# Strassen loop of a two-mixer kernel: token preparation gets call places of its own, masked rows a step of their own

## The chip, the cores and the metric

The kernel runs on one core of a Trainium2 chip. The metric is the device time of one execution in microseconds (us). TensorE is written PE (its weight loads PEld), VectorE DVE, ScalarE ACT, GpSimd POOL and SyncE SP.

## The reference

Pooled attention, then two mixers, over 8 batches of 576 tokens with 512 channels:

```python
attn = softmax(q @ mean8(k).T / 8) @ mean8(v)
x = attn laid out as (8, 576, 512)
u = x + (x.T @ U @ V).T
x1 = u + relu(u @ w1a) @ w2a
u2 = x1 + real(fft(fft(x1, axis=tokens), axis=channels))
un = (u2 - mean(u2)) / sqrt(var(u2) + 1e-6)
out = u2 + relu(un @ w1b) @ w2b
```

All of it is held to float32 precision: the matmuls take operands split into a high and a low part (`hi`, `lo`), so one product takes two or three matmuls.

## The kernel before

An opening and a first loop do attention, the first mixer's low-rank part and six of the nine 512-token blocks of its feed-forward layer. Then comes the **Strassen loop**, at line 1592: twelve blocks `seq[k]`, three of the first feed-forward layer (phase 0) and nine of the second (phase 1), with `NPR` = 8 turns `p` each, so 96 turns. A turn makes the seven Strassen products of one pair of 128-column slices of the hidden layer and the second layer of the turn before (`prev`). PE's order within a turn is written out by hand: products 0 and 1, `st2_a(prev, 0)`, `tick(0)`, products 2 and 3, `st2_a(prev, 1)`, `tick(1)`, products 4 and 5, `st2_a(prev, 2)`, `tick(2)`, product 6, `st2_a(prev, 3)`, `tick(3)`. The even products go to PSUM bank `h0`, the odd ones to `h1`, and DVE and ACT empty a bank before the next product may write it.

DVE's own work of a turn has a fixed order: `sa<-h,sa` after product 1 (product 3 waits for it), `hl<-sb` for the second layer, `sb<-h,sb` after product 4 (product 6 waits for it), `sa<-h,sa`, `sb<-sb`, `sa<-sa`, then `sb<-sa` and `hl<-sa` after product 6. PE, ACT and DVE run in program order (`manual_schedule`); SP and POOL are ordered by the scheduler.

Other work is cut into steps by Python generators, called lanes. `step(name)` (line 1346) runs one lane to its next `yield`, and what it issues stands at that place of every engine's queue. Two lanes run in the Strassen loop:

- `d`, the spectral lane (`lane_d`, `Dft.run`, line 747): the two Fourier transforms of one batch, residual and normalisation. A batch is twelve steps that form sums and differences of rows (three row groups, four steps each), one that masks the last rows (line 841) and in the same step makes the first stage group on PE (`stage`, seven matmuls), three with a further stage group, two for the extra column `px`, one with the first group of the second transform (`second`, thirteen matmuls), and for each of two or three row groups: differences (`S`, `E`), four additions (lines 940 to 943), two `bn_stats` (line 964), mean and variance, reciprocal root and first scaling, second scaling with the next `second`. Batch 0 runs in the first loop, batches 1 to 7 in the Strassen loop. After each pair of batches `state["u2"]` says how many rows of `un` are there.
- `p`, the preparation of the next block's operands (`prep_a`, line 1074): three steps that issue loads (`ul`, four DMAs each), five that transpose a tile on DVE (line 1122), copy high parts on ACT (line 1071) and subtract low parts on DVE (line 1072, shown as L121), then six with additions and subtractions for the Strassen operands, and a last one with two subtractions: fifteen calls.

`tick(i)` calls `swap()` (which replaces the second-layer weights, turns 17 to 31), one step of `d` and one of `p`. `place()` in `prep_a` lets the lane rest at `tick(2)`, once its loads are issued, so the preparation has three working calls a turn, at ticks 0, 1 and 3. It begins at the top of turn 0 of a block, or the first later turn at which `ready_for(k + 1)` holds; at turn 6 `until` runs all lanes until the preparation is done. In turn 0 DVE also adds the residual of the block just finished (`ur`, four additions, one behind each `st2_a`).

Of the kernel before, what the change touches and what calls it, by code (L numbers as in the profile page):

```python
# [61 lines left out]
def kernel(  # L62
# [663 lines left out]
    class Dft:  # L726
# [20 lines left out]
        def run(self, b, group):  # L747
# [47 lines left out]
            for i in range(3):  # L795
                f, r, n = fr
                if i < 2 and two():
                    fr = loads(i + 1)
                if low:
                    low()  # L800
                s = tl("S")
                e = tl("E")
                add(nc.vector, s[:n], f[:n], r[:n])
                yield
                sub(nc.vector, r[:n], f[:n], r[:n])
                nc.gpsimd.tensor_copy(e[:n, 0:1], s[:n, 0:1])
                nc.gpsimd.memset(e[:n, 511:512], 0.0)
                yield
                sub(nc.vector, e[:n, 256:511], r[:n, 1:256], r[:n, 256:511])
                add(nc.vector, e[:n, 1:256], s[:n, 1:256], s[:n, 256:511])  # L810
                if i < 2 and fr[0] is f:
                    fr = loads(i + 1)
                yield
                c2 = s[:n, 511:512].to_broadcast([n, 64])
                xe = tl(f"xe{i}", (128, 96 if i < 2 else 64), F32R)
                if i < 2:
                    xh, xl = tl(f"xh{i}", dt=F32R), tl(f"xl{i}", dt=F32R)
                    nc.scalar.activation(out=xh, in_=e, func=ACTF.Copy)
                    nc.scalar.activation(out=xe[:, 0:64], in_=c2, func=ACTF.Copy)

                    def low(xh=xh, xl=xl, xe=xe, e=e, c2=c2):
                        sub(nc.vector, xl, e, xh.bitcast(F32))
                        sub(nc.vector, xe[:, 64:96], c2[:, 0:32], xe[:, 0:32].bitcast(F32))
                    X.append((xh, xl))
                    XE.append(xe)
                    yield
                    if not two():
                        low()
                        low = None
                        yield  # L830
                else:
                    m = self.sm
                    both = []
                    for h, y, q in ((xe, c2, f[:, 0:64]), (None, e, r)):
                        h = h or tl("S", dt=F32R)
                        nc.scalar.activation(out=h[:n], in_=y[:n], func=ACTF.Copy)
                        nc.vector.tensor_scalar(out=q[:n], in0=y[:n], scalar1=m[:n, 0:1], scalar2=None, op0=ALU.mult)
                        both.append((h, q))
                    yield
                    for h, q in both:  # L840
                        nc.vector.scalar_tensor_tensor(out=h[:n], in0=h[:n].bitcast(F32), scalar=m[:n, 1:2], in1=q[:n], op0=ALU.mult, op1=ALU.add)  # L841
                    X.append((h,))
                    XE.append(xe)
            P = []
            if slot == 0:
                self.cat = (tl("cath", (128, 4, 99), F32R), tl("catl", (128, 4, 99), F32R), tl("catp", (96, 99), F32R))
# [84 lines left out]
            for i in range(n2):  # L931
                f, r, n = fr
                yield
                s = tl("S")
                sub(nc.vector, s[:n, 0:257], a[:n, 0:257], e[:n, 0:257])
                add(nc.vector, e[:n, 0:257], a[:n, 0:257], e[:n, 0:257])
                if i + 1 < n2 and two():
                    fr = loads2(i + 1)
                yield
                add(nc.vector, f[:n, 0:256], f[:n, 0:256], s[:n, 0:256])  # L940
                add(nc.vector, f[:n, 256:512], f[:n, 256:512], e[:n, 1:257])
                add(nc.vector, r[:n, 0:256], r[:n, 0:256], e[:n, 0:256])
                add(nc.vector, r[:n, 256:512], r[:n, 256:512], s[:n, 1:257])

                def rows(o, f, r):
                    if i < 2:
                        k0 = KT[i][0]
                        nc.sync.dma_start(out=o[z + k0:z + k0 + n, :], in_=f[:n])
                    if i == 0:
                        for a, m in ((1, 15), (16, 112)):  # L950
                            nc.sync.dma_start(out=o[z + 288 + a:z + 288 + a + m, :], in_=r[a:a + m])
                    elif i == 1:
                        nc.sync.dma_start(out=o[z + 416:z + 544, :], in_=r)
                    else:
                        for j, zj in enumerate(y * S for y in group):
                            nc.sync.dma_start(out=o[zj + 256:zj + 289, :], in_=f[33 * j:33 * j + 33])
                            nc.sync.dma_start(out=o[zj + 544:zj + 576, :], in_=r[33 * j:33 * j + 32])
                rows(u2d, f, r)
                yield
                ms = p1.tile([128, 2, 2], F32, tag="mv", name="mv", bufs=2)  # L960
                rs = p1.tile([128, 2, 2], F32, tag="rs", name="rs", bufs=2)
                bs = [p1.tile([128, 6], F32, tag="bs", name="bs", bufs=2) for _ in range(2)]
                for x, st in zip((f, r), bs):
                    nc.vector.bn_stats(out=st[:n], in_=x[:n])  # L964
                yield
                for g, st in enumerate(bs):
                    nc.vector.bn_aggr(out=ms[:n, g], in_=st[:n])
                v, y, t = ms[:n, :, 1], rs[:n, :, 0], rs[:n, :, 1]
                nc.vector.tensor_scalar(out=v, in0=v, scalar1=1e-6, scalar2=None, op0=ALU.add)
                nc.gpsimd.tensor_tensor(out=y, in0=v, in1=mhalf[:n, 0:1].to_broadcast([n, 2]), op=ALU.pow)  # L970
                yield
                nc.vector.tensor_tensor(out=t, in0=y, in1=y, op=ALU.mult)
                nc.vector.tensor_tensor(out=t, in0=t, in1=v, op=ALU.mult)
                nc.vector.tensor_scalar(out=t, in0=t, scalar1=-0.5, scalar2=1.5, op0=ALU.mult, op1=ALU.add)
                nc.vector.tensor_tensor(out=y, in0=y, in1=t, op=ALU.mult)
                again = two()
                un = [pools[1].tile([128, DM], F32, tag=x, name=x) for x in ("S2", "E2")] if again else (s, e)

                def scale(g):
                    x = (f, r)[g]  # L980
                    nc.vector.tensor_scalar(out=un[g][:n], in0=x[:n], scalar1=ms[:n, g, 0:1], scalar2=rs[:n, g, 0:1], op0=ALU.subtract, op1=ALU.mult)
                scale(0)
                yield
                scale(1)
                rows(und, *un)
                if i + 1 < n2:
                    if fr[0] is f:
                        fr = loads2(i + 1)
                        yield
                        yield  # L990
                        yield
                    a, e = second(i + 1, fr[2])
                elif again and b + 1 < B and state["x1"] >= (b + 2) * S:
                    self.ahead[b + 1] = loads(0, (b + 1) * S)
# [79 lines left out]
    def prep_a(i):  # L1074
# [18 lines left out]
                fn()  # L1093
            z.clear()

        def place():
            while state["tick"] == 2:
                yield

        def highs(t, ms, src):  # L1100
            for h, m in ms:
                if m not in x:
# [1 line left out]
                low.append(op_split(x[m], t % 2, quarter(src, h)))  # L1104

        for t in range(n + 1):
            yield from place()
            old = low
            low = []
            if t:  # L1110
# [17 lines left out]
            x["s2"], x["s4"] = optile(), optile()  # L1128
        for i in range(2):
            a11, a12, a21, a22 = [z.rearrange("p (a x) -> p a x", a=4)[:, :, 64 * h:64 * h + 64] for z in (r[i], r[2 + i]) for h in range(2)]  # L1130
            yield from place()
            flush(low)
            add(nc.vector, a22, a21, a22)
            sub(nc.vector, a21, a11, a21)
            yield
            yield from place()
            sub(nc.vector, a11, a22, a11)
            sub(nc.vector, a12, a12, a11)
            yield
            yield from place()  # L1140
            highs(i, ((1, "s1"), (0, "s3")), r[2 + i])
            if first:
                highs(i, ((0, "s2"), (1, "s4")), r[i])
            yield
        yield from place()
        flush(low)
        if not first:
            late_ops.update(s2=[quarter(r[i], 0) for i in range(2)], s4=[quarter(r[i], 1) for i in range(2)])
# [429 lines left out]
        nc.scalar.activation(out=o, in_=src, func=ACTF.Copy)  # L1578

    def tick(i):  # L1580
        state["tick"] = i
        swap()
        for name in ("d", "p"):
            step(name)

    def ready_for(k):
        phase, b = seq[k]
# [4 lines left out]
    for k in range(len(seq)):  # L1592
        begun = k + 1 == len(seq)
        for p in range(NPR):
            x = ops[k]
            n = 7 * (NPR * k + p)
            end = p == NPR - 1 and k + 1 < len(seq)
            if not begun and ready_for(k + 1):
                begun = True
                lanes["p"] = prep_a(k + 1)  # L1600
            o, v = two(bank("h0")), two(bank("h1"))
# [5 lines left out]
                high1 = hi_of(1, prev[3])  # L1607
            product(n + 1, v, x["a12"], True, False)
            add(nc.vector, a[:, :, 0], v, a[:, :, 0])
            if prev:  # L1610
                st2_a(prev, 0)
                prev[2].append((high1, lo_of(1, high1, prev[3])))
# [6 lines left out]
            b = mq.tile([128, 2, 256], F32, tag="sb", name="sb")  # L1619
            product(n + 3, v, x["s1"], True, False)  # L1620
            copy(b, v)
            if prev:
                st2_a(prev, 1)
            lows = late_op(k, "s4") if end else []
# [136 lines left out]
```

## Time and profile before

| | us |
|---|---|
| median of 3 executions | 1798.95 |
| lowest and highest | 1797.61, 1801.49 |
| the profiled execution, its own time | 1800.14 |
| its span, first to last instruction | 1798.4 |
| PE busy in the span | 1767.0 |
| DVE busy in the span | 1158.2 |

Times in rows are microseconds from the start of the span unless marked ns. A row of a timeline has start, busy time, engine, line, operation, what it writes and reads, and in brackets the idle time of the engine before it with what ended it. A row of a list of waits has the engine, line and what it waited for, then the total, the number of times and the longest. PE's busy time counts a matmul from start to a modelled end, and matmuls overlap.

### The profile page before, as it was taken

The page shows a single profiled execution, that of the slowest core. Times are in us where ns is not written, and L with a number is a line of the kernel's source. Part 1 is how long each engine was busy: PE and PEld are TensorE (multiplying, and loading weights), DVE is VectorE, ACT ScalarE, POOL GpSimd, SP SyncE. Part 2 cuts the span into 40 slices and gives each one's busy share as a digit, 9 for nine tenths or more (in the row PEclk, how much of TensorE's full clock was granted, in tenths as well). Part 3 has the DMA queues.
Part 4 walks back from the last instruction along what each step waited for, and adds up shares of the span by engine and source line. Part 5 has one row for each costly group of instructions (what it writes and reads, how often), then busy time and mean ns, then how long its engine had stood idle before and what let it go on. Part 6 is the DMA issues. An engine that isn't in the chain of part 4 may idle for free.

```text
span 1798.4 us, 27008 instructions
## 1 busy us (share of the span) xinstructions
PE 1767.0 (98%) x8928; PEld 1491.8 (83%) x8928; DVE 1158.2 (64%) x2382; ACT 796.4 (44%) x2013; POOL 223.0 (12%) x357
## 2 busy tenths in 40 slices
PE   8999999999999999999999999999999999999999
PEld 7878888888888888788888788888888888888887
DVE  7567665565444335868687968688786765656544
ACT  7675455665554122434344434443443343433332
POOL 3443423323100000000000000000000000000000
PEclk9999999999999999999999999999999999999999
DMA  9538687777674414868597968778686876767663
GB/s 350 222 100 256 229 267 244 253 255 252 213 230 146 143 51 148 272 212 284 186 316 238 299 208 261 236 245 263 214 277 200 252 231 196 230 192 246 193 201 117
DMA packets 260268, 401.19 MB, mean 223 GB/s; under 512 B 23808, under 2 KB 89568, under 8 KB 260128
## 3 DMA queue, kind: packets, MB, share of 16 engines
q1 hardware_dynamic: 259408, 396.82, 69.2%
q0 software_dynamic: 720, 2.65, 0.4%
q8 instruction: 71, 1.16, 0.3%
q14 instruction: 69, 0.57, 0.1%
HBM read 311.55 MB, written 87.82 MB: 222 GB/s over the span
## 4 chain that ended last, share of the span: by engine, by line
PE 68%; DVE 6%; DMA 2%; issue 1%; ACT 1%; SPq 0%; POOL 0%; DVEq 0%; ACTq 0%; POOLq 0%
PE h L139 32%; PE o L139 17%; PE m L139 8%; PE hu L139 6%; PE s L139 5%; DVE sa L124 1%; DMA R<-x1d 1%; DMA wr<-wc 1%; DVE sb L124 1%; DVE hl L1574 1%; DVE ur L124 0%; DVE bs L964 0%; DVE S L841 0%; SPq L1002 0%; DVE ul L1122 0%
## 5 line engine op out<-in xcount | busy, mean ns | idle before, releaser
L139 PE MATMUL h<-x,wr 128*128 128x512 f32 (+1 forms) x2688 | 537.9, 339 | 9.1 <-DVE sa L124 5.7
L139 PEld LDWEIGHTS h<-x,wr 128*128 128x128 f32 x2688 | 408.9, 190 | 66.6 <-DVE sa L124 7.3
L1578 ACT ACTIVATE sa<-h 128x512 f32<-128x512 f32 x288 | 172.7, 600 | 495.0 <-PE h L139 428.7
L139 PE MATMUL o<-w,hh 128*128 128x512 f32 x1152 | 328.8, 393 | 0.0
L139 PE MATMUL h<-utx,w 128*128 128x512 f32 x1152 | 282.6, 393 | 3.0 <-DVE hl L1201 1.4
L139 PEld LDWEIGHTS h<-utx,w 128*128 128x128 f32 x1152 | 213.7, 188 | 49.6 <-POOL w L121 2.5
L139 PEld LDWEIGHTS o<-w,hh 128*128 128x128 f32 x1152 | 214.5, 188 | 46.5 <-ACT hh L1569 0.3
L139 PE MATMUL o<-w,hl 128*128 128x512 f32 x576 | 193.9, 391 | 0.0
L1201 DVE SCALAR_TENSOR_TENSOR hl<-h,hh 128x512 fp32r<-128x512 f32 x96 | 66.3, 691 | 177.8 <-ACT hh L1196 177.3
L139 PE MATMUL m<-w,hh 128*128 128x512 f32 x576 | 163.1, 391 | 0.0
L124 DVE TENSOR_TENSOR sa<-h,sa 128x512 f32<-128x512 f32 x192 | 131.5, 685 | 45.0 <-PE h L139 42.9
L124 DVE TENSOR_TENSOR sb<-h,sb 128x512 f32<-128x512 f32 x96 | 66.0, 687 | 140.5 <-PE h L139 140.2
L139 PEld LDWEIGHTS m<-w,hh 128*128 128x128 f32 x576 | 108.2, 188 | 24.5
L139 PEld LDWEIGHTS o<-w,hl 128*128 128x128 f32 x576 | 108.4, 188 | 23.8
L1196 ACT ACTIVATE hh<-h 128x512 fp32r<-128x512 f32 x96 | 57.4, 598 | 151.6 <-PE h L139 151.6
L139 PE MATMUL hu<-w,hh 128*128 128x512 f32 x384 | 103.7, 391 | 0.0
L656 ACT ACTIVATE s<-s,mx 128x72 f32<-128x72 f32 x280 | 82.2, 331 | 36.8 <-DVE mx L652 36.7
L139 PE MATMUL m<-w,hl 128*128 128x512 f32 x288 | 96.7, 390 | 0.0
L124 DVE TENSOR_TENSOR sb<-sa 128x256 f32<-128x256 f32 x96 | 40.7, 424 | 71.0 <-ACT sa L1578 70.8
L139 PEld LDWEIGHTS hu<-w,hh 128*128 128x128 f32 x384 | 72.1, 188 | 16.8
L121 POOL TENSOR_TENSOR wo<-wo 128x256 fp32r<-128x256 f32 x88 | 65.2, 755 | 127.2 <-ACT wo L135 82.0
L1574 DVE SCALAR_TENSOR_TENSOR hl<-sa,hh 128x512 fp32r<-128x512 f32 x96 | 66.4, 692 | 6.7
(264 smaller groups left out, 2541.6 us busy)
## 6 DMA issues: line engine op xcount, KB each, us to landing
wr<-wc SPq DMA_DIRECT2D x336, 512.0 KB
wc<-wo SPq DMA_DIRECT2D x88, 256.0 KB
x<-x SPq DMA_DIRECT2D x48, 256.0 KB
ur<-ud SPq DMA_DIRECT2D x36, 256.0 KB
x1d<-ur SPq DMA_DIRECT2D x36, 256.0 KB
ul<-und SPq DMA_DIRECT2D x144, 64.0 KB
ur<-u2d SPq DMA_DIRECT2D x36, 256.0 KB
out<-ur SPq DMA_DIRECT2D x36, 256.0 KB
```

The lines of the kernel that those rows point to most:

```text
L121: eng.tensor_tensor(out=o, in0=a, in1=b, op=ALU.subtract)
L124: eng.tensor_tensor(out=o, in0=a, in1=b, op=ALU.add)
L139: nc.tensor.matmul(o, a, b, start=start, stop=stop, skip_group_check=True)
L656: nc.scalar.activation(out=s[:, a], in_=v[:, k], func=ACTF.Exp, bias=mx[:, a:a + 1], **kw)
L1196: nc.scalar.activation(out=hh, in_=o, func=ACTF.Relu)
L1201: nc.vector.scalar_tensor_tensor(out=hl, in0=o, scalar=0.0, in1=hh.bitcast(F32), op0=ALU.max, op1=ALU.subtract)
L1574: nc.vector.scalar_tensor_tensor(out=hl, in0=r, scalar=0.0, in1=hh.bitcast(F32), op0=ALU.max, op1=ALU.subtract)
L1578: nc.scalar.activation(out=o, in_=src, func=ACTF.Copy)
```

## The change

The masked rows end with a `yield`, so the first stage group moves to the next step of `d`. `place()` goes. `tick` calls `d` four times a turn as before, and `p` at tick 1 alone, where no step of `d` since tick 0 was marked heavy (the four additions and the `bn_stats`). Two calls of `p` are added that depend on nothing: one right behind `sa<-h,sa` of product 1, one right behind the copy of product 3. The preparation begins at turn 1 at the earliest.

```diff
@@ -841,6 +841,7 @@
                         nc.vector.scalar_tensor_tensor(out=h[:n], in0=h[:n].bitcast(F32), scalar=m[:n, 1:2], in1=q[:n], op0=ALU.mult, op1=ALU.add)
                     X.append((h,))
                     XE.append(xe)
+                    yield
             P = []
             if slot == 0:
                 self.cat = (tl("cath", (128, 4, 99), F32R), tl("catl", (128, 4, 99), F32R), tl("catp", (96, 99), F32R))
@@ -941,6 +942,7 @@
                 add(nc.vector, f[:n, 256:512], f[:n, 256:512], e[:n, 1:257])
                 add(nc.vector, r[:n, 0:256], r[:n, 0:256], e[:n, 0:256])
                 add(nc.vector, r[:n, 256:512], r[:n, 256:512], s[:n, 1:257])
+                state["heavy"] = True
 
                 def rows(o, f, r):
                     if i < 2:
@@ -962,6 +964,7 @@
                 bs = [p1.tile([128, 6], F32, tag="bs", name="bs", bufs=2) for _ in range(2)]
                 for x, st in zip((f, r), bs):
                     nc.vector.bn_stats(out=st[:n], in_=x[:n])
+                state["heavy"] = True
                 yield
                 for g, st in enumerate(bs):
                     nc.vector.bn_aggr(out=ms[:n, g], in_=st[:n])
@@ -1093,10 +1096,6 @@
                 fn()
             z.clear()
 
-        def place():
-            while state["tick"] == 2:
-                yield
-
         def highs(t, ms, src):
             for h, m in ms:
                 if m not in x:
@@ -1104,7 +1103,6 @@
                 low.append(op_split(x[m], t % 2, quarter(src, h)))
 
         for t in range(n + 1):
-            yield from place()
             old = low
             low = []
             if t:
@@ -1128,21 +1126,17 @@
             x["s2"], x["s4"] = optile(), optile()
         for i in range(2):
             a11, a12, a21, a22 = [z.rearrange("p (a x) -> p a x", a=4)[:, :, 64 * h:64 * h + 64] for z in (r[i], r[2 + i]) for h in range(2)]
-            yield from place()
             flush(low)
             add(nc.vector, a22, a21, a22)
             sub(nc.vector, a21, a11, a21)
             yield
-            yield from place()
             sub(nc.vector, a11, a22, a11)
             sub(nc.vector, a12, a12, a11)
             yield
-            yield from place()
             highs(i, ((1, "s1"), (0, "s3")), r[2 + i])
             if first:
                 highs(i, ((0, "s2"), (1, "s4")), r[i])
             yield
-        yield from place()
         flush(low)
         if not first:
             late_ops.update(s2=[quarter(r[i], 0) for i in range(2)], s4=[quarter(r[i], 1) for i in range(2)])
@@ -1578,10 +1572,12 @@
         nc.scalar.activation(out=o, in_=src, func=ACTF.Copy)
 
     def tick(i):
-        state["tick"] = i
+        if i % 2 == 0:
+            state["heavy"] = False
         swap()
-        for name in ("d", "p"):
-            step(name)
+        step("d")
+        if i == 1 and not state["heavy"]:
+            step("p")
 
     def ready_for(k):
         phase, b = seq[k]
@@ -1595,7 +1591,7 @@
             x = ops[k]
             n = 7 * (NPR * k + p)
             end = p == NPR - 1 and k + 1 < len(seq)
-            if not begun and ready_for(k + 1):
+            if not begun and p and ready_for(k + 1):
                 begun = True
                 lanes["p"] = prep_a(k + 1)
             o, v = two(bank("h0")), two(bank("h1"))
@@ -1607,6 +1603,7 @@
                 high1 = hi_of(1, prev[3])
             product(n + 1, v, x["a12"], True, False)
             add(nc.vector, a[:, :, 0], v, a[:, :, 0])
+            step("p")
             if prev:
                 st2_a(prev, 0)
                 prev[2].append((high1, lo_of(1, high1, prev[3])))
@@ -1619,6 +1616,7 @@
             b = mq.tile([128, 2, 256], F32, tag="sb", name="sb")
             product(n + 3, v, x["s1"], True, False)
             copy(b, v)
+            step("p")
             if prev:
                 st2_a(prev, 1)
             lows = late_op(k, "s4") if end else []
```

## Rows read from the trace of the kernel before

**Rows 1.** The page's busy time by engine: us, share of the span, instructions

```profile
PE 1767.0 (98%) x8928; PEld 1491.8 (83%) x8928; DVE 1158.2 (64%) x2382; ACT 796.4 (44%) x2013; POOL 223.0 (12%) x357
```

**Rows 2.** Windows: busy us (instructions) of PE, PEld, DVE, ACT, POOL, granted clock, DMA share, GB/s

```profile
1500.00:1600.00 100.00, 100.00 (x503) 84.80 (x502) 58.28 (x110) 37.70 (x73) 0.00 (x0) 1.00 0.69 210
1024.20:1027.70 3.50, 3.50 (x12) 2.86 (x11) 2.40 (x10) 0.46 (x1) 0.62 (x1) 0.51 0.98 359
```

**Rows 3.** Waits of PE, 700 us to the end

```profile
PE h L139 <- DVE sa L124: 5.7, 6, 2.0
PE s L139 <- DVE S L841: 4.5, 7, 1.0
PE h L139 <- DVE sb L124: 1.8, 4, 0.7
PE h L139 <- ACT sa L1578: 1.5, 1, 1.5
```

**Rows 4.** Waits of PE, whole span

```profile
PE s L139 <- DVE S L841: 6.0, 8, 1.5
```

**Rows 5.** Line 1569: ns least/median/most, first and last start; one a turn

```profile
L1569 ACT ACTIVATE hh<-sa x96: 621/624/627, 721.8 to 1788.3; 128x512 fp32r<-128x512 f32 x96
```

**Rows 6.** Timeline of ACT, the same instruction in four turns

```profile
781.80 0.62 ACT L1569 ACTIVATE hh<-sa 128x512 fp32r<-128x512 f32 x1
793.75 0.62 ACT L1569 ACTIVATE hh<-sa 128x512 fp32r<-128x512 f32 x1
...
955.05 0.62 ACT L1569 ACTIVATE hh<-sa 128x512 fp32r<-128x512 f32 x1
968.96 0.62 ACT L1569 ACTIVATE hh<-sa 128x512 fp32r<-128x512 f32 x1
```

**Rows 7.** Timeline of a turn without spectral work and preparation, from product 0

```profile
1508.88 1.56 PE L139 MATMUL h<-x,wr 128*128 128x512 f32 x8
...
1511.16 0.68 DVE L1574 SCALAR_TENSOR_TENSOR hl<-sb,hh 128x512 fp32r<-128x512 f32 x1
...
1516.95 0.69 DVE L124 TENSOR_TENSOR sa<-sa 128x512 f32<-128x512 f32 x1
...
1517.18 0.86 PE L139 MATMUL h<-x,wr 128*128 128x256 f32 x4
...
1519.26 1.56 PE L139 MATMUL h<-x,wr 128*128 128x512 f32 x8
...
1522.02 1.56 PE L139 MATMUL h<-x,wr 128*128 128x512 f32 x8
```

**Rows 8.** Timeline around the longest wait of PE in the loop

```profile
1016.38 0.68 DVE L121 TENSOR_TENSOR w<-w 128x512 fp32r<-128x512 f32 x1
...
1018.32 0.42 DVE L124 TENSOR_TENSOR sb<-sa 128x256 f32<-128x256 f32 x1
...
1019.26 0.69 DVE L121 TENSOR_TENSOR w<-w 128x512 fp32r<-128x512 f32 x1
...
1021.06 0.74 DVE L121 TENSOR_TENSOR x<-ul,x 128x256 fp32r<-128x256 f32 x2
...
1022.35 0.65 DVE L124 TENSOR_TENSOR sa<-h,sa 128x512 f32<-128x512 f32 x1
...
1023.05 0.97 PE L139 MATMUL h<-x,wr 128*128 128x256 f32 x4 [1.99 <-DVE sa L124]
```

**Rows 9.** Timeline of one masked step and its stage group

```profile
861.75 0.75 DVE L841 SCALAR_TENSOR_TENSOR S<-S,smk,R 99x512 fp32r<-99x512 f32 x1
...
862.55 0.40 PE L139 MATMUL s<-st,S 99*128 99x290 f32 x1 [0.97 <-DVE S L841]
```

**Rows 10.** Tile ul, from 700 us: engines idle before its instructions until (us, times)

```profile
  ACT x L1071: 11.4, 8
  DMA ul<-ud: 2.4, 1
```

**Rows 11.** Line 964 from 600 us: ns least/median/most, first and last start

```profile
L964 DVE BATCH_NORM_STATS2 bs<-F x20: 654/687/690, 674.1 to 1416.1; 128x6 f32<-128x512 f32 x16, 66x6 f32<-66x512 f32 x4
```

## The prediction, made before the changed kernel ran

> **What bounds the kernel now.** I read the busy times by engine, then PE's list of waits, the windows of the loop, and the timeline around single waits. PE is busy 98% of the span, DVE 64% [rows 1], so time can only come from PE's gaps. A late window of the loop, without spectral work, shows none: PE busy 100 of 100 us [rows 2]. From 700 us on the list of waits names four things: two DVE additions that empty banks (5.7 and 1.8 us), the masked rows (4.5 us in seven waits) and one copy of ACT (1.5 us) [rows 3], 13.5 us together. An eighth wait for masked rows, of 1.5 us, lies in the first loop (6.0 less 4.5) [rows 3, 4].
>
> The gaps shown are not all that is lost. The loop can be measured by an instruction that comes once a turn: 95 turns take 1788.3 less 721.8, or 1066.5 us [rows 5]. A turn alone takes 10.38 us, from product 0 to product 0 [rows 7], so 95 take 986.1. The spectral matmuls are real work: a turn with one group of the second transform takes 11.95 us, 1.57 more, and one with three stage groups and the `px` group 13.91, 3.53 more [rows 6]. Seven batches have 7 x 3.53 = 24.7; their fourth stage group, 7 of the 26 matmuls of such a turn, is 0.95 each, 6.7; the 18 groups of the second transform (four batches with three, three with two) are 28.3. Together 59.7. So 1066.5 - 986.1 - 59.7 = **20.7 us are lost**. The period is read to a hundredth, which is 1 us in the sum.
>
> Idle shown and time lost differ by 7 us. One reason is visible: behind the longest wait, 1.99 us [rows 8], the granted clock was 0.51 for 3.5 us, the 1.2 GHz level [rows 2], which loses about 1.7. The rest I put down to matmuls that overlap, so that part of a stall hides under a busy time. The Trainium skill (Perfetto Trace Analysis, section Identifying the Most-Contended Engine) says the same in general: busy time of matmuls is no good measure of the room left, because they are pipelined. By the busy time alone the loop would have 13.5 us to give, by the turns 20.7; I go by the turns.
>
> **Why PE waits.** DVE works in program order and has two open stretches a turn. The first goes from the addition behind product 1 (the next instruction starts at 1511.16) to the latest start of the `sb` addition that frees the bank for product 6 (1517.18 less its 0.69): 5.33 us, less 0.60 for `hl`, leaves **4.73** [rows 7]. The second goes from the end of `sa<-sa` (1516.95 and 0.60) to the latest start of the addition that product 3 waits for. Product 3 begins half way through eight matmuls, about 0.7 after 1522.02, so the addition must start by 1522.03. That is 4.48, less 0.34 and 0.60 for DVE's two own instructions: **3.54** [rows 7]. Back to back, a 512-wide instruction takes 0.60 (three in 1.80), a 256-wide one 0.34 (0.60 and four of them in 1.94), two subtractions and a transpose 1.29, so a transpose 0.62 [rows 8].
>
> At the longest wait the second stretch held 1.94 us (a weight swap and four additions at tick 2) and 3.09 at tick 3: a swap and two `bn_stats` 1.80, the preparation's subtractions and transpose 1.29 [rows 8]. That is 5.03 against 3.54, 1.5 too much, and DVE entered late besides; PE waited 1.99. The second stretch is the short one, and the preparation's call at tick 3 fills it.
>
> **The change, part by part.**
>
> *No preparation at tick 3.* The second stretch keeps `d` alone: at most 1.34 and 1.20 (additions, `bn_stats`), 2.54, against 3.54; with two swaps, in turns 17 to 31 alone, 3.74, 0.2 over. Turn 0 adds two `ur` there (1.20), and no longer a transpose. The waits for `sa` and the slow clock behind the longest go, and the `sb` wait at turn 1, which stood behind a transpose that waited 2.4 for its load [rows 10], goes too.
>
> *Two new calls and tick 1, all in the first stretch.* The fifteen calls cost DVE 0, 0, 0, 0.62, 0.62, 1.29, 1.29, 0.34, 1.02, 0.68, 0, 1.36, 0.68, 0, 0.68. Three in a row hold 3.20 at most (from the fifth), mostly 2.5 to 2.9. That leaves 1.5 to 2.2 of the 4.73 for `d` at ticks 0 and 1. Most pairs of `d` steps need 0.8 to 1.6; the pair of two subtractions, a sum and a difference (0.60, 0.2, 0.60 and 0.60) needs 2.0, and a swap adds 0.60. A heavy pair needs 2.54, but then tick 1 makes no preparation: at worst 2.58 at the two new places, 5.12 against 4.73. So the worst turn is 1.1 over (3.20 + 2.0 + 0.6 - 4.73), and such turns come at most once a block: 0 to 8.6 us over eight blocks beside spectral work. I take **2.5**, since most combinations fit.
>
> Behind the call at the first place DVE's queue holds `hl<-sb`, which the second layer uses some 4 us later; behind the one at the second place, `d` at tick 1 and the `sb` addition, counted above. On ACT two 0.3 us copies come ahead of the copy of product 2, in an engine 44% busy [rows 1]; inside the 0 to 8.6.
>
> *Beginning at turn 1.* Twelve calls at the two places in turns 1 to 6 and six at tick 1, of which heavy steps can block three (a batch has at most three pairs of heavy steps, and the next pair is a batch away): 15, just what is needed, so `until` finds nothing to do. The sixteen `ul` loads of a block move about a turn later on SP, and each transpose comes a full turn, over 10 us, after its load; before, one transpose of eleven blocks waited [rows 10]. Cost nothing; the cover is that turn.
>
> *Masked rows apart.* The stage group moves one tick on, over 2 us (product 6 and a quarter of the second layer at the least), against waits of 0.97 [rows 9] and at most 1.5 [rows 4]. All eight waits go. The lane grows by eight steps, two turns. Its last `bn_stats` starts at 1416.1 [rows 11]; the block that needs the last pair is prepared from turn 65, 30 turns before the end at 1788.3, so near 1477. Room for two turns is there.
>
> **Sum.** 20.7 lost, less 1.5 for the ACT copy at the loop's start, which is untouched, plus 1.5 in the first loop, less 2.5 new: 18.2 us. The profiled execution took 1800.1, 1.2 above the median; 1781.9 there, **1781** as a median.
>
> **The rivals.**
>
> *Only what the gaps show comes back.* DVE's waits 7.5, masked rows 6.0, clock 1.7, less 2.5: 12.7, so 1786; with the bound of 8.6 in place of 2.5, 1792. For it: the difference of 7 us is attributed, not seen. Against: the sum over turns has no free term. Chance 0.18.
>
> *The preparation is not kept from heavy steps.* The flag is read at tick 1 alone; the two new places look at nothing, so the text of the change holds only in part. If that and the fuller first stretch give PE waits on `sb` in two turns of each of eight blocks at 1.1, 17.6 return: 20.7 - 17.6 is 3.1, so 1796. Against: needs the worst turn throughout. Chance 0.06 (same).
>
> *ACT and DVE hand over in the first stretch (slower).* A subtraction at tick 1 needs a high part that ACT copies at the place before, behind the copy of product 3, and the `sb` addition stands behind it. If DVE idles there in two turns of each of eleven blocks, 22 times, the gain is gone from 0.94 us each; before, such waits were 11.4 us in 8, 1.4 each [rows 10]. At 1.4 net, 30.8 come back: 1809. For it: it is the one wait that the change brings nearer to PE. Against: the copies can be done about 0.7 after the copy of product 3, and subtractions and transpose then need 1.3, inside the slack of 1.1 behind the usual start. Chance 0.08.
>
> **How the numbers follow.** The forecast, 1777 to 1785, has 0.68; the first rival, up to 1792, 0.18. Faster by over 0.2% (3.6 us, about what a measurement can tell here) is their sum, 0.86; same 0.06; slower 0.08. The range starts at 1776 (no new waits, and a little of the period's hundredth) and ends at 1790, inside the first rival.
>
> **What would show it.** Right: no row of PE waiting for line 841; `sa` waits gone; the once-a-turn instruction spanning about 1048 us; clock 1.0 through the loop; no transposes at tick 3. Wrong: new waits of PE on `sb` or on `hl`, DVE idle for ACT's copies, or a turn 6 with an `until`.

## The result, and the profile of the changed kernel

The changed kernel takes **1780.22 us** (median of 4 runs, 1779.74 to 1780.66) where the kernel before, beside it, takes 1798.92: a ratio of 0.9894, 95% interval 0.9882 to 0.9906. The profiled execution took 1780.13, its span is 1778.3. All times of the experiments below are read against the kernel before on their own chip, 1798.73 to 1798.93. Every kernel here computes all of the reference.

Three views of the changed kernel answer to those of before. The page's busy time by engine, as [rows 1]:

```profile
PE 1759.0 (99%) x8928; PEld 1490.2 (84%) x8928; DVE 1161.4 (65%) x2382; ACT 792.5 (45%) x2013; POOL 217.3 (12%) x357
```

PE's list of waits from 690 us to the end, as [rows 3] (total, times, longest):

```profile
PE h L139 <- ACT sa L1572: 3.4, 4, 1.5
```

The instruction that comes once a turn, now line 1563, as [rows 5]:

```profile
L1563 ACT ACTIVATE hh<-sa x96: 619/624/625, 719.0 to 1768.3; 128x512 fp32r<-128x512 f32 x96
```

Three of the four rows of [rows 3] are gone: no DVE addition and no masked row is waited for. The loop takes 1768.3 - 719.0 = 1049.3 us where it took 1066.5. The two profiled executions are 20.0 us apart (1800.14 less 1780.13; the medians are 18.7 apart), and **17.2 of them came in the loop**, 2.8 ahead of it. The work of the loop alone, 986.1 + 59.7 = 1045.8 us by the prediction, is called the **floor** below. Against it the loop had lost 20.7 and now loses 3.5; the waits shown were 13.5 and are 3.4, so the gap of 7 us between lost and shown has closed too. PE's busy time fell by only 8.0 and its share rose from 98 to 99%: the page alone would hardly have told this gain.

Tile `ul` of the changed kernel from 690 us, as [rows 10]:

```profile
  ACT x L1074: 33.6, 27
```

DVE now idles 33.6 us in 27 places for ACT's copies, where it was 11.4 in 8, and PE's list names none of it: there is no row of PE waiting for `sb`. All 27 lie in the first stretch. Eleven of them, 12 us, stand beside spectral work; the other 16 come behind 1430 us, where the spectral lane has ended and the turns keep to 10.37 or 10.38 us.

What is left over is one copy of ACT, four times. One of them, 1.5 us, is at the loop's start as before; the longest of the others, a timeline of the changed kernel in turn 21:

```profile
950.89 0.25 DVE L837 TENSOR_SCALAR F<-S,smk 99x64 f32<-99x64 f32 x1
951.05 0.48 DVE L837 TENSOR_SCALAR R<-E,smk 99x512 f32<-99x512 f32 x1
951.25 0.63 ACT L836 ACTIVATE S<-E 99x512 fp32r<-99x512 f32 x1 [2.94 <-DVE F L837]
951.79 0.58 ACT L1572 ACTIVATE sa<-h 128x512 f32<-128x512 f32 x1
...
952.42 1.69 PE L139 MATMUL h<-x,wr 128*128 128x512 f32 x8 [1.35 <-ACT sa L1572]
```

ACT stands 2.94 us before it may write the rounded masked rows into tile `S`, since DVE's `F<-S` still reads what lay in that tile. ACT works in program order, and behind that instruction is the copy that empties product 2's bank; product 4 wants the bank and PE waits 1.35.

### The profile page after: what moved, and what is told of

Read it like the earlier page. It is cut to its first block, busy times and chain, and to the rows that moved or that the text cites. A ratio compares the mean times of both kernels' runs of the same rounds, so it can differ in the third digit from the quotient of the medians.

```text
span 1778.3 us, 27034 instructions
## 1 busy us (share of the span) xinstructions
PE 1759.0 (99%) x8928; PEld 1490.2 (84%) x8928; DVE 1161.4 (65%) x2382; ACT 792.5 (45%) x2013; POOL 217.3 (12%) x357
## 4 chain that ended last, share of the span: by engine, by line
PE 74%; DVE 1%; issue 1%; ACT 1%; DMA 0%; POOL 0%; ACTq 0%; POOLq 0%; DVEq 0%
PE h L139 34%; PE o L139 18%; PE m L139 9%; PE hu L139 8%; PE s L139 5%; DMA w<-wd 0%; DVE sa L124 0%; PE s L664 0%; ACT sa L1572 0%; DVE hl L1568 0%; DVE x L121 0%; ACT S L836 0%; POOL wo L121 0%; DVE sb L124 0%; DVE w L121 0%
## 5 line engine op out<-in xcount | busy, mean ns | idle before, releaser
L121 DVE TENSOR_TENSOR x<-ul,x 128x256 fp32r<-128x256 f32 x154 | 59.0, 418 | 33.6 <-ACT x L1074 33.6
```

The source lines that it names most:

```text
L121: eng.tensor_tensor(out=o, in0=a, in1=b, op=ALU.subtract)
```

## The experiments

The prediction put the gain on DVE's second stretch (preparation at tick 3) and on the masked waits. The experiments take the parts apart. e1 to e12 are their labels; their edits are cut to the lines that change. Loop lengths are the once-a-turn instruction's last start less its first; "lost" is the length less 1045.8; "shown" is the sum of PE's waits from 690 us. Each comes from one profiled execution. Two kernels were traced twice, and their loops repeat closely: 1049.28 and 1049.30 (changed, e8), 1046.69 and 1046.69 (e7, e11). The medians scatter by more, since the part ahead of the loop differs by 0.8 and 1.5 us between these same traces. A turn of 10.38 us is a little long: 33 quiet turns of the kernel before, from 1435.59 to 1777.91, take 10.373 each, so the floor is some 0.6 too high and every "lost" 0.6 too low. Differences between rows don't change by that.

| kernel | median | ratio, 95% | loop | lost | shown |
|---|---|---|---|---|---|
| before | 1798.9 | | 1066.5 | 20.7 | 13.5 |
| e6, preparation off tick 3 | 1797.02 | 0.9993 (0.9984–1.0003) | 1064.5 | 18.7 | 12.5 |
| e10, one empty step of `d` a batch | 1792.09 | 0.9964 (0.9951–0.9976) | 1060.9 | 15.1 | 10.5 |
| e2, all but the masked rows' step | 1791.12 | 0.9962 (0.9947–0.9977) | 1058.2 | 12.4 | 10.3 |
| e1, the masked rows' step alone | 1786.76 | 0.9940 (0.9925–0.9955) | 1055.3 | 9.5 | 6.9 |
| e12, e1 and the edit of e6 | 1786.77 | 0.9934 (0.9920–0.9949) | 1055.0 | 9.2 | 6.9 |
| e9, e1 and beginning at turn 1 | 1783.35 | 0.9914 (0.9900–0.9929) | 1052.3 | 6.5 | 4.0 |
| e4, changed, no look at heavy | 1782.51 | 0.9906 (0.9891–0.9921) | 1050.5 | 4.7 | 3.2 |
| e8, changed, once more | 1780.96 | 0.9895 (0.9880–0.9909) | 1049.3 | 3.5 | 3.5 |
| e3, changed, beginning at turn 0 | 1780.65 | 0.9896 (0.9879–0.9914) | 1049.9 | 4.1 | 4.3 |
| e5, changed, third call at tick 3 | 1780.75 | 0.9896 (0.9881–0.9911) | 1050.3 | 4.5 | 4.4 |
| e7, changed, own tile for masked rows | 1777.36 | 0.9887 (0.9871–0.9904) | 1046.7 | 0.9 | 1.6 |
| e11, the same | 1776.93 | 0.9880 (0.9866–0.9895) | 1046.7 | 0.9 | 1.6 |

**The two halves, e1 and e2.** e1 is the kernel before with the new step of the masked rows and nothing else; e2 is the changed kernel without it.

```diff
                     X.append((h,))
                     XE.append(xe)
+                    yield
```

> The kernel before with the masked rows' own step alone. Theory (two full stretches of DVE, time counted by turns): all eight waits of PE on line 841 go, the waits on the sa and sb additions and the slow-clock stretch stay, since the preparation still has its call at tick 3. By turns a masked row's stage costs 0.65 us in four batches and 1.3 in three, 6.4, and about 1.5 in the first loop: 1791 us (1788 to 1794). Rival (only the gaps shown come back): 6.0 us, 1793. Rival (what counts is how the two lanes fall together, and the extra step shifts them): the waits on sa and sb change by several us either way, 1784 or 1798.

> The changed kernel without the masked rows' own step: the preparation's places alone. Theory: the waits on line 841 stay (6.0 us in eight), the waits on sa and sb and the slow clock go: 20.7 less 1.5 less 6.4, 12.8, less about 2 of new waits in the first stretch: 1787 to 1789. Rival (gaps only): 7.5 and 1.7, less 2: 1792. Together with the run of the masked rows alone the two gains should add up to the 18.7 us of the whole change within 2 us; if they don't, the parts act on each other.

The one line gives 12.0 of the 18.7 us, all else alone 7.6; together 19.6, so they overlap by about 1. One `yield` was worth twice the masked waits it removes [rows 4]. For e1 the theory missed (1788 to 1794 expected, 1786.8 measured); its last rival, the shift of the lanes, named the size but not the way. e2, at 1791.1, lies between its theory and its rival. e1's once-a-turn row and its waits of PE:

```profile
L1570 ACT ACTIVATE hh<-sa x96: 622/624/627, 718.8 to 1774.1; 128x512 fp32r<-128x512 f32 x96
```

```profile
PE h L139 <- DVE sb L124: 3.4, 5, 1.7
PE h L139 <- ACT sa L1579: 1.8, 2, 1.5
PE h L139 <- DVE sa L124: 1.7, 4, 0.6
```

The masked row is gone, and so is 4.0 of the 5.7 of `sa`, although the preparation stands at tick 3 as before; `sb` has gained 1.6. In e2, where it has left tick 3, the masked row is even longer than in [rows 3]:

```profile
PE s L139 <- DVE S L841: 6.4, 7, 1.6
PE h L139 <- DVE sa L124: 1.8, 3, 0.6
PE h L139 <- ACT sa L1571: 1.5, 1, 1.5
PE h L139 <- DVE sb L124: 0.6, 2, 0.4
```

**Tick 3 by itself, e6 and e12.** e6 moves one of the preparation's calls from tick 3 to the place behind product 1, in the kernel before; e12 does so on top of e1.

```diff
-        for name in ("d", "p"):
-            step(name)
+        step("d")
+        if i < 2:
+            step("p")
...
             add(nc.vector, a[:, :, 0], v, a[:, :, 0])
+            step("p")
```

> The kernel before with one call of the preparation moved: from tick 3 to the place behind the addition of product 1; ticks 0 and 1 keep theirs, it begins at turn 0 as before, nothing looks for heavy steps, masked rows as before. Theory (the second stretch was the short one): the waits on sa and the slow clock go, some waits on sb come since the first stretch is the fuller one: 8 to 12 us faster, 1787 to 1791. Rival (the gain of the places comes from beginning at turn 1, away from the four residual additions, or from the heavy check): under 5 us, above 1794.

> The kernel before with the masked rows' own step and the call at tick 3 moved behind product 1; it begins at turn 0, calls beside heavy steps. Theory C (either remedy is enough): 1780 to 1783. Theory D (the first stretch is as scarce as the second, so a move alone is worth the 1.7 us it brought without the masked step): 1784 to 1787.

e6 gives 1.7 us with an interval that holds 1, where 8 to 12 were expected; e12 gives nothing beyond e1, as its theory D has it. Moving the call from tick 3 into the first stretch is worth next to nothing by itself. The waits of PE in e6 say why:

```profile
PE s L139 <- DVE S L841: 3.5, 6, 1.0
PE h L139 <- DVE sb L124: 3.1, 7, 0.9
PE h L139 <- DVE sa L124: 2.0, 3, 0.7
PE h L139 <- ACT sa L1578: 1.5, 1, 1.5
PE h L139 <- DMA wr<-wc: 1.4, 2, 1.1
PE s L139 <- DMA wr<-wc: 1.0, 1, 1.0
```

`sa` falls from 5.7 to 2.0, as the prediction's second stretch has it, but `sb`, at the end of the first stretch, rises from 1.8 to 3.1, and waits for weight loads by DMA appear. In e12 the waits for `sb` are 4.0. Turn 9 of e1 and of e12 shows such a first stretch, in a timeline of DVE and PE:

```profile
817.37 0.70 DVE L1123 STREAM_TRANSPOSE ul<-ul 128x512 f32<-128x512 f32 x1
...
819.82 0.70 DVE L1123 STREAM_TRANSPOSE ul<-ul 128x512 f32<-128x512 f32 x1
820.45 0.65 DVE L124 TENSOR_TENSOR sb<-h,sb 128x512 f32<-128x512 f32 x1
...
821.15 0.97 PE L139 MATMUL h<-x,wr 128*128 128x256 f32 x4 [0.41 <-DVE sb L124]
```

```profile
815.39 0.70 DVE L1123 STREAM_TRANSPOSE ul<-ul 128x512 f32<-128x512 f32 x1
...
820.37 0.70 DVE L1123 STREAM_TRANSPOSE ul<-ul 128x512 f32<-128x512 f32 x1
821.00 0.65 DVE L124 TENSOR_TENSOR sb<-h,sb 128x512 f32<-128x512 f32 x1
...
821.70 0.97 PE L139 MATMUL h<-x,wr 128*128 128x256 f32 x4 [0.41 <-DVE sb L124]
```

The first is e1, the second e12. In both the heavy pair of `d`, that is the four additions and the `bn_stats`, stands at ticks 0 and 1 beside two transposes of the preparation. In e12 a third transpose leads the stretch; from it to `sb` are 5.61 us, and the prediction's room, `hl` included, was 5.33. In e1 that transpose stands at tick 3, just ahead of the addition that opens the stretch, and DVE comes as late: the wait is 0.41 us in both. So the first stretch does overflow where a heavy pair falls on the turn of the transposes, and moving one call across its border changes nothing there.

**The empty step, e10.** If the new step does more than take the masked waits away, a step that does nothing should show it. e10 is the kernel before with a second `yield` ahead of the masked arithmetic; masked rows and stage group stay in one step.

```diff
                     yield
+                    yield
                     for h, q in both:
```

> The kernel before with an empty step of the spectral lane ahead of the masked rows: as many steps as with the masked rows' own step, so the lanes fall together in the same way, but the stage group stays with the masked rows. Theory (masked waits and shift add): the eight waits on line 841 stay at 5 to 8 us, the slow-clock stretch and part of the waits on sa go as in the run of the masked rows alone, 1793 to 1796, so that 3 to 6 of its 12 us are the shift. Rival (all 12 us are the masked waits): 1798 to 1800.

It gives 6.8 us and does no work; 3 to 6 were expected. Its once-a-turn row and its waits:

```profile
L1570 ACT ACTIVATE hh<-sa x96: 619/624/627, 718.6 to 1779.5; 128x512 fp32r<-128x512 f32 x96
```

```profile
PE s L139 <- DVE S L842: 3.5, 7, 1.0
PE h L139 <- DVE sb L124: 3.4, 5, 1.7
PE h L139 <- DVE sa L124: 1.8, 4, 0.6
PE h L139 <- ACT sa L1579: 1.8, 2, 1.5
```

e10 and e1 have lanes of the same length, and below the masked row their lists agree to a tenth. Between them lies the masked row alone: 3.5 us shown, 5.6 in the loop (1060.9 less 1055.3), 5.3 in the median. The other half of e1's gain, 5.6 in the loop, is the **shift**: every later step of `d` stands one tick on for each batch gone by, and other spectral steps meet the preparation. The `sa` waits fall by 3.9, those for `sb` rise by 1.6, and the 1.99 us wait with its stretch at half clock [rows 2, 8], about 1.7 of the 5.6, does not come up in this execution. Ahead of the loop the eighth masked wait is gone as well.

Turn 8 of the kernel before shows a meeting that the shift undoes, in a timeline of DVE and PE:

```profile
819.68 0.68 DVE L964 BATCH_NORM_STATS2 bs<-R 66x6 f32<-66x512 f32 x1
820.27 0.69 DVE L1122 STREAM_TRANSPOSE ul<-ul 128x512 f32<-128x512 f32 x1
820.88 0.65 DVE L124 TENSOR_TENSOR sa<-h,sa 128x512 f32<-128x512 f32 x1
...
821.59 0.98 PE L139 MATMUL h<-x,wr 128*128 128x256 f32 x4 [1.17 <-DVE sa L124]
```

Here the heavy pair stands at ticks 2 and 3, with a transpose behind it, and `sa` is late. In e10 and e1 the same pair stands two ticks on, at ticks 0 and 1 of turn 9, and it is `sb` that is late, by 0.41. Read turn by turn, five of the six `sa` waits before (5.3 of 5.7 us) come behind a second stretch that holds a heavy step and a transpose. In e10 no second stretch does; five first stretches do, and they are its five waits for `sb`. In the changed kernel neither stretch does in any turn. The loss follows that meeting, and not tick 3 as such.

What was not tried is other shifts (two empty steps, or one elsewhere). Whether this one is a lucky phase or most phases are better than that of before stays open; that the time depends on it by 6.8 us is shown.

**What is left for the places: e9, e3, e4, e5.** e9 adds to e1 the beginning at turn 1; e3, e4 and e5 take single parts of the changed kernel back.

```diff
e9, on e1:
+            if not begun and p and ready_for(k + 1):
e3:
-            if not begun and p and ready_for(k + 1):
+            if not begun and ready_for(k + 1):
e4:
-        if i == 1 and not state["heavy"]:
+        if i == 1:
e5:
+        if i == 3 and not state["heavy"]:
```

(e5's line takes the place of the one that e4 shows removed.)

> The kernel before with the masked rows' own step and the preparation beginning at turn 1; its calls stay at ticks 0, 1 and 3, beside heavy steps too. The run of the masked rows alone took 1786.8; its waits on sb and sa fall in the turns behind turn 0 of a block, where the residual additions, spectral steps and a transpose at tick 3 meet. Theory C (two remedies for one collision: either a later beginning or no call at tick 3 is enough): 1780 to 1783. Theory D (the places behind products 1 and 3 are needed): 1784 to 1787.

> The changed kernel, but the preparation may begin at turn 0 as before (three calls of loads there, transposes from turn 1 on). The move of one call alone brought 1.7 us where 8 to 12 were expected. Theory A (the later beginning and the heavy check carry the rest): waits on sa and sb come back around turns 0 to 2 of the blocks, 4 to 8 us slower than the changed kernel, 1784 to 1788. Theory B (what counts is that ticks 2 and 3 are free of the preparation and that the steps of both lanes fall together by luck): within 2 us, 1779 to 1782.

> The changed kernel with the preparation's call at tick 1 in every turn, beside heavy steps too. Theory A: 2 to 5 us slower, waits on sb in turns where the four additions or the bn_stats stand at ticks 0 and 1: 1782 to 1785. Theory B (a heavy pair with three calls is 2.5 and 2.9 against 4.7 us, but the preparation's full turns fall elsewhere): 0 to 1.5 us, 1779 to 1782.

> The changed kernel with the third call of a turn at tick 3 (unless a heavy step stood at tick 2 or 3) in place of tick 1. Theory of the second stretch (3.54 us, which the call at tick 3 overfills): waits on sa come back, 1.29 and 1.36 us of preparation beside d steps of 1.2 to 2.0: 3 to 6 us slower, 1783 to 1786. Rival (the first stretch is as scarce, so it gains what the second loses): 1779 to 1782.

> The changed kernel once more, on the same chip and between the same runs as its three variants, so that they are compared with it and not across chips: 1780.2 within 1.5.

e9 is 3.4 us below e1 and 3.1 above the changed kernel (2.4 above e8), between its two theories. Its turn 9, in which e1 and e12 wait, in a timeline of DVE:

```profile
819.76 0.69 DVE L124 TENSOR_TENSOR sb<-h,sb 128x512 f32<-128x512 f32 x1 [0.72 <-PE h L139]
```

The heavy pair is still there, the transposes have gone to a later turn, and DVE waits for PE instead. The `sb` row is gone from the list of waits, `sa` stays:

```profile
PE h L139 <- ACT sa L1579: 2.4, 2, 1.5
PE h L139 <- DVE sa L124: 1.6, 8, 0.4
```

So beginning later does keep the transposes from the heavy pair of that turn. Inside the changed kernel, though, taking it back costs nothing in the median (e3 -0.3 against e8, theory B) and 0.6 in the loop; nor does a third call at tick 3 instead of tick 1 cost more (e5 -0.2, its rival; 1.0 in the loop). Without the look at heavy steps it is 1.6 (e4, theory A just so; 1.2 in the loop; its four runs, 1782.43 to 1782.97, all above e8's highest, 1781.29). The parts stand in for one another: the collision wants one remedy, and the change has several.

**A tile of its own, e7 and e11.** The left-over waits are put down to ACT standing before tile `S`. e7 gives the masked rows a tile of their own in the Strassen loop, and nothing else.

```diff
+                        if h is None and two():
+                            h = pools[1].tile([128, DM], F32R, tag="S2", name="S2")
                         h = h or tl("S", dt=F32R)
```

> The changed kernel with the rounded copy of the masked rows in a tile of its own (S2) and not in the tile S that DVE still reads. In the changed kernel PE waits 3.4 us for the copy sa of ACT, 1.5 of it at the loop's start; the rest falls in turns where ACT stands before its copy into S until DVE has read S (line 837). Theory: those 1.9 us go, 1.5 stay: 1778 us, 0.1% faster than the changed kernel. Rival: the wait moves to the next thing that DVE is late with, no change, 1780.

> The changed kernel with a tile of its own for the rounded masked rows, again: 1777.4 in the first run against 1780.2 and 1781.0 of the changed kernel. If the 3 us are more than chance: 1776 to 1779. If not: 1780.

Waits of PE and once-a-turn row of e7:

```profile
PE h L139 <- ACT sa L1574: 1.6, 2, 1.5
```

```profile
L1565 ACT ACTIVATE hh<-sa x96: 621/622/627, 718.5 to 1765.2; 128x512 fp32r<-128x512 f32 x96
```

1777.36, and 1776.93 in the repeat, as its theory has it: 2.9 to 4.0 us below the changed kernel's two medians (1780.22 and, in e8, 1780.96). The waits fall to the one of 1.5 at the loop's start and 0.1 more; the loop's 1046.7 is 0.9 over the floor, or 1.5 with the period of 10.373. This is the fastest version here, below both kernels.

## Why the prediction was right, and where its working was not

**The sum.** 1781 was forecast and 1780.22 measured. The loop was to span "about 1048" and spans 1049.3; that figure took all 18.2 off the loop, though 1.5 of them lie ahead of it, and the sum's own terms give 1049.8. Counting by turns decided it. "Only what the gaps show comes back" would have given 1786: the waits fell by 10.1 us, the loop by 17.2, and that rival is out. The remaining 7.1 us were real and came back with the waits; about 1.7 of them belong to the slow clock, the rest is loss that the list of waits doesn't show. In the traced execution of e10, which has no slow stretch in its loop, it is 4.6 (15.1 lost, 10.5 shown). The prediction put it down to matmuls that overlap, and a timeline of the kernel before bears that out, one masked wait beside the same matmuls without one:

```profile
952.72 0.30 PE L139 MATMUL s<-st,xl 128*128 128x290 f32 x1
953.41 0.40 PE L139 MATMUL s<-st,S 99*128 99x290 f32 x1 [0.40 <-DVE S L841]
953.65 0.86 PE L139 MATMUL h<-x,wr 128*128 128x256 f32 x4
...
956.40 0.29 PE L139 MATMUL s<-st,xl 128*128 128x290 f32 x1
956.53 0.29 PE L139 MATMUL s<-st,S 99*128 99x290 f32 x1
956.66 1.57 PE L139 MATMUL h<-x,wr 128*128 128x512 f32 x8
```

Without a wait these matmuls start 0.13 us apart, though each is listed with 0.29. With it they start 0.69 and 0.24 apart: 0.67 us lost where 0.40 is shown, 0.27 hidden. The 0.41 us wait of e1's turn 9 hides as much (0.68 lost, against the same matmuls in a turn without it). By an estimate from these two, the 18 waits of [rows 3] hide 4.9 us, and e10's 18 the same; with the slow clock that is most of the 7.1. The rule of the Trainium skill that the busy time of matmuls is no good measure (Perfetto Trace Analysis, section Identifying the Most-Contended Engine) agrees with these numbers. Its reason, that pipelined matmuls look smaller in the trace, is another than the one seen here, where overlapping listed times hide part of a stall; so the prediction's "says the same" holds for the rule alone.

**Masked rows apart.** All eight waits went, as forecast. The two numbers behind it were off: the seven in the loop are worth 5.6 where e10's list shows 3.5 (e10 to e1), and "the lane grows by eight steps", costed at nothing but room at its end, was itself worth 5.6 in the loop (e10; about 3.9 without the slow stretch). **This is the step that failed**: the working asked whether the lane still ends in time, and not which steps of `d` meet which calls of `p` once each has moved by a tick.

**No preparation at tick 3.** "The second stretch is the short one, and the preparation's call at tick 3 fills it" is right for the turn it was read from [rows 8], and `sa` falls when the call leaves (e6). As the account of the gain it fails: e6 gives 1.7, e12 nothing, and e5 keeps a call there at no cost in the median. The working laid 7.5 us of waits, the slow clock and the unseen loss to it. In the order e10, e1, e9, changed, the loop's 17.2 us are 5.6 for the shift, 5.6 for the masked waits, 3.0 for the later beginning, 3.0 for the places and the look at heavy steps together. Other orders share it out otherwise: places and beginning are worth 8.3 without the masked step (e2) and 6.0 behind it. Two errors of opposite sign, the shift at nothing and tick 3 at too much, left the sum right. The total was counted down from a floor and needed only that nearly all the loss goes, not by which part; that it went although the account of the parts was wrong is luck.

**The two new places.** 2.5 of new waits were taken, in the first stretch, on `sb`. No wait on `sb` came; 1.9 (3.4 less the 1.5 at the loop's start) came instead on ACT's copy, from a tile that the working did not look at. Near in size by luck, wrong in place; e7 shows the cause by removing it. That turns overflow the first stretch at all is seen in e12.

**Preparation not kept from heavy steps.** As its condition says, the two places look at nothing; but the worst turn did not come. e4 shows what the look at tick 1 is worth: 1.6.

**ACT and DVE hand over (slower).** Its condition came true almost to the number: 30.8 us of DVE's idle time in 22 places were priced, and 33.6 came in 27. PE's list shows no cost of it: DVE had slack there, which was the argument against it, and most of it came where no spectral work is left. What 33.6 us of one engine's idle time cost another can't be read from their sum.

**Ahead of the loop.** 1.5 was taken for the first loop's masked wait; the first turn's mark stands at 719.0 instead of 721.8, 2.8 sooner. Kernels with the new step, e10's empty one too, have it at 718.2 to 720.0, e2 at 721.7; e6, which changes nothing there, at 720.2. Two traces of one kernel differ there by 0.8 (changed, e8) and 1.5 (e7, e11). So about half of the 2.8 may be scatter.

## What to carry to other kernels

Measure a loop that is bound by one engine with an instruction that comes once a turn, against a quiet turn's period and the extra work: the gaps shown were 13.5 of the 20.7 us that could be had. Where lanes are cut into steps and woven by a fixed order, an added step shifts all behind it; run the edit as an empty step first, to tell the shift from the work. In the trace, look for the turns in which long steps of two lanes meet, and not only for the place where one call stands. And where an engine runs in program order, look for what stands behind an instruction that waits for a tile to come free: here a copy that PE needed, 3 us for one more tile.

## What the runs showed of the hardware that was not expected

- A wait of PE need not be followed by a slower clock. In the kernel before a wait of 1.99 us was followed by 3.5 us at a granted clock of 0.51, the 1.2 GHz level [rows 2, 8]; in e12 a longer wait, 2.25 us, was followed by 3.5 us at 1.00, the 2.4 GHz level (a row of a timeline, and a window with the columns of [rows 2]; the clock is the third number from the end):

```profile
1006.70 0.97 PE L139 MATMUL h<-x,wr 128*128 128x256 f32 x4 [2.25 <-DVE sb L124]
```

```profile
1006.70:1010.20 3.50, 3.50 (x17) 2.81 (x18) 3.46 (x10) 1.64 (x4) 0.79 (x1) 1.00 1.02 389
```

- Nor need the same kernel meet the slower stretch each time. Of 29 executions of the kernel before beside e1 to e12, 14 have a mean granted clock of 1.000 (median 1798.0 us) and 15 one of 0.999 or 0.998 (median 1799.9). A mean doesn't say where the stretch lay. The shift is more than that: among executions at 1.000 on one chip, the kernel before takes 1798.0 and e10 1791.7.
